# Attention's transposes moved from VectorE to the DMA queue, and the down/wo weight sums made in place inside the first gate/up pass

## Chip, cores and metric

The kernel runs on 1 core of one Trainium2 chip. The metric is device time in microseconds (us), the median over runs. Before the change it is 732.66 us, the median of 6 runs (731.0 to 733.2).

## What is computed

A gated mix of two branches over 2048 tokens of width 1024. `B` is a gated feed-forward block (hidden width 3584). `A` is a sliding, dilated attention: 32 heads of 32, each token looks at 8 keys, 0, 2, ..., 14 positions back. A sigmoid gate per token mixes them. Cut to what matters:

```python
def _A_ref(x, wqkv, wo):
    H = 32; Dh = D // H; W, dil = 8, 2
    q, k, v = split_heads(x @ wqkv)
    idx = pos[:, None] - (jnp.arange(W) * dil)[None, :]
    mask = idx >= 0
    logits = jnp.einsum("bhsd,bhswd->bhsw", q, k[idx]) * Dh ** -0.5
    attn = softmax(jnp.where(mask, logits, -1e9))
    o = jnp.einsum("bhsw,bhswd->bhsd", attn, v[idx])
    return merge_heads(o) @ wo

def _B_ref(x, w_gate, w_up, w_down):
    return (gelu(x @ w_gate) * (x @ w_up)) @ w_down

g = sigmoid((x * gate_w).sum(-1, keepdims=True))
out = g * _A_ref(x, wqkv, wo) + (1 - g) * _B_ref(x, w_gate, w_up, w_down)
```

## The kernel before

**Tiling.** The 2048 tokens are four chunks of 512 (`SC`); two chunks form a "sup". For each sup the program runs a gate/up pass (`ffn`, L963: 28 tiles of 128 hidden columns, taken two at a time as 14 blocks) and then a down stage for each of its chunks (`down`, L1063 and `down_rest`, L1136). In between stands the q, k, v projection of the next sup's chunks (`qkv_pair`); the first two chunks are projected at the start (`qkv_outer`, `qkv`). The large products are made by a scheme of seven half-size products instead of eight (Strassen's, in Winograd's form), in pairs of chunks or halves. It needs sums and differences of the operands beforehand: of the gate/up weights (`wforms`, L427), of x (`x_forms`), of the projection weights (`qkv_forms`), of the down and wo weights (`preps`, L402) and of h (`forms`, L1095), all made by VectorE. The sums of down and wo weights are stored to DRAM (`dforms`, `oforms`) by DMAs on the POOL queue and read back in each down stage; the gate/up sums are used at once and also stored (`fforms`) for the second sup.

**Attention.** It has no matmuls besides the projections. A chunk is taken as two halves of 256 tokens, so there are eight halves, `h` = 0 to 7. `scores` (L765) multiplies q by eight shifted views of k on VectorE and adds over eight tiles: eight products (L781) and seven adds (L787), each of 128 x 2048 bf16. `att_half` (L818) then has partial sums with the head's channels on the partitions. It transposes them (L844), folds the four remaining channels (L851, L854), takes the softmax over the eight window positions (L867 to L898, with the exponential on ScalarE, L880), spreads the weights back over channels on ScalarE (L904), transposes back in two pieces (L913), multiplies by eight shifted views of v (L922) and sums over the window (L930, L935, L939). The result overwrites q in `qo` and is the left operand of the wo product in the down stage. The transposes are VectorE's, by blocks of 32 x 32, so that a partition after the transpose holds one token of a group of 32 and 8 heads; the gate's per-token values `ez` and the mask follow that layout (`SB`, `HQ`, L861).

Five buffers `xbuf` (128 x 2048 bf16) serve all of it. The products of half `h` wait until the transpose of half `h`-1 is done (`acct`, L772).

**Weights.** `ring` has 20 slots of 256 KB. Every weight piece is loaded into the next free slot by a DMA on SP's queue; a slot is free when the last matmul on it is done. SP issues strictly in order: `loads` (L366) is the list. A block of the first gate/up pass takes four loaded pieces and four sums, a block of the second seven loads, a product of the down stage nine pieces.

**The order.** `Weave` (L41) puts several generators (`main`, `loads`, `wforms`, `preps`, `attention`, `scores` and others) into one order for each engine when the program is built: it keeps a clock per engine, gives every operation a written cost, and always emits the operation that could start first, plus a small bias per generator (L1255). The order is fixed then; each engine works through its own list and waits at whichever operation isn't ready. A DMA is taken to end when its bytes have passed a pipe of 340 GB/s and 2.2 us more have gone (L90 to L93). The operations of `main` stay in order among themselves.

**`preps` and its staging.** Nine rounds: seven for the down weights, two for wo. A round loads four 256 KB pieces (`load_prep`, L316), makes four differences of 128 x 1024 (L409 to L414), and stores four pieces (L419). The loads go to one of five areas in rows 8 to 27 of `hT`, the results to the next area (L405). `hT` is the hidden activation (28 rows), which the gate/up pass fills from row 0 up; rows from 8 on wait until all of `preps` is stored (L1030). The loads of all nine rounds stand before block 2's in the list.

Of the kernel before, what the change touches and what calls it, by code (L numbers as in the profile page):

```python
# [9 lines left out]
ALU = mybir.AluOpType  # L10
# [30 lines left out]
class Weave:  # L41
# [42 lines left out]
    def _emit(self, op, t):  # L84
        cost = op.cost
        if op.eng == "ACT" and op.table is not None and op.table != self.table:
            self.table = op.table
            cost += 1.29
        if op.eng in ("SP", "POOL"):
            nbytes, issue = op.cost  # L90
            self.clk[op.eng] = t + issue
            self.pipe = max(self.pipe, t) + nbytes / self.RATE
            op.end = self.pipe + 2.2  # L93
        else:
            self.clk[op.eng] = t + cost
            op.end = t + cost + op.tail
        instructions = self.nc.cur_bb.bb.instructions
        n0 = len(instructions)
        op.fn()
        for ins in self.nc.cur_bb.bb.instructions[n0:]:  # L100
            eng = getattr(ins, "engine", None)
            if eng is None or not getattr(ins, "name", None) or type(ins).__name__.startswith("BassTile"):
                continue
            prev = self.last.get(eng)
            if prev is not None:
                self.tc.add_manual_dep(ins, prev, mybir.DependencyInfo(mybir.DependencyClass.NoSync,
                                                                      mybir.DependencyReason.DATA),
                                       reason="engine order")
            self.last[eng] = ins.name
            self.names.append((ins.name, len(self.log)))  # L110
        if op.key is not None:
            self.done[op.key] = op
        self.log.append((op.eng, t, op.end, op.key, op.fn.__qualname__.split(".")[2], op.cost))
# [23 lines left out]
def kernel(  # L137
# [31 lines left out]
    SB = AC // 32  # L169
    HQ = 32 // DL  # L170
# [126 lines left out]
    NPREP = FH + NTH  # L297
    def stage(i):
        f0 = 8 + 4 * i
        return hT[:, :, f0:f0 + 4, :].rearrange("p (a b) f s -> p a b (f s)", b=2)  # L300
# [14 lines left out]

    def load_prep(i0):  # L316
        n = min(2, NPREP - i0)
        kind, src, nr = ("d", B_w_down, FH) if i0 < FH else ("o", A_wo, NTH)
        r0 = i0 if kind == "d" else i0 - FH
        si = i0 % 5  # L320

        def fn():
            st = stage(si)
            for h, r in ((0, r0), (1, nr + r0)):
                if kind == "d":
                    v = src[r * P:(r + n) * P, :].rearrange("(k p) (h n) -> p k h n", p=P, h=2)
                else:
                    v = AP(src.tensor, src.offset + r * D, [[NT * D, P], [D, n], [NW, 2], [1, NW]])
                for k in range(n):
                    nc.sync.dma_start(out=st[:, 2 * h + k], in_=v[:, k])  # L330
        return Op("SP", (4 * n * P * NW * 2, 2.0 * n), fn, [("preps", i0 - 6)] if i0 >= 6 else [], key=("prep", i0))
# [34 lines left out]
    def loads():  # L366
# [5 lines left out]
                 [("pt", NST - 1, 1)], key=("wqkv", 0, 2))  # L372
        yield load_prep(2)
        yield from load_x(1, [])
        for i0 in (4, 6, 8, 10):
            yield load_prep(i0)
        yield from load_block(0, 0)
        yield load_prep(12)
        yield from load_block(0, 1)
        for i0 in (14, 16):  # L380
            yield load_prep(i0)
        for b in range(2, NBLK):
            yield from load_block(0, b)
            if b >= XB:
                for c, k0 in ((2, 0), (2, 4), (3, 0), (3, 4))[b - XB:b - XB + 1]:
                    yield from list(load_x(c, []))[k0:k0 + 4]
# [15 lines left out]
    def preps():  # L402
        for i0 in range(0, NPREP, 2):
            kind, r0, n = ("d", i0, min(2, FH - i0)) if i0 < FH else ("o", i0 - FH, min(2, NPREP - i0))
            st, ot = stage(i0 % 5), stage((i0 + 1) % 5)  # L405
            b11, b12, b21, b22 = st[:, 0:n, 0], st[:, 0:n, 1], st[:, 2:2 + n, 0], st[:, 2:2 + n, 1]
            fo = ot[:, :, 0:n, :]
            t = tt(n * NW)
            f0 = dve(t, lambda: V(out=fo[:, 0], in0=b12, in1=b11, op=ALU.subtract), [("prep", i0)], lag=1.0)  # L409
            yield f0  # L410
            yield dve(t, lambda: V(out=fo[:, 2], in0=b22, in1=b12, op=ALU.subtract))
            f1 = dve(t, lambda: V(out=fo[:, 1], in0=b22, in1=fo[:, 0], op=ALU.subtract), [f0])
            yield f1
            last = dve(t, lambda: V(out=fo[:, 3], in0=b21, in1=fo[:, 1], op=ALU.subtract), [f1])  # L414
            yield last
            dd = (ddram if kind == "d" else odram)[:].rearrange("f p (k n) -> p f k n", n=NW)
            for f in range(4):
                o = Op("POOL", (n * P * NW * 2, 0.8),
                       lambda f=f: nc.gpsimd.dma_start(out=dd[:, f, r0:r0 + n, :], in_=fo[:, f]), [last],  # L419
# [289 lines left out]
    def gate(c):  # L709
# [20 lines left out]
        ez = small.tile([P, SC // 32], F32, tag="ez", bufs=2, name="ez")  # L730
        omg = small.tile([P, NST], F32, tag="omg", bufs=3, name="omg")
        gates[c] = (ez, omg, zq)

    def gate_sum(c):
        i, free = bank_take()
        zq = gates[c][2]

        def go():
            for q in range(4):
                nc.tensor.matmul(banks[i][32 * q:32 * (q + 1), 0:SC // 32], lhsT=qsum[:], rhs=zq[:], start=True, stop=True,  # L740
# [3 lines left out]
        e = dve(0.1, lambda: nc.vector.tensor_scalar(out=zq[:], in0=banks[i][:, 0:SC // 32], scalar1=ZMAX, scalar2=-ZMAX,  # L744
# [4 lines left out]
    def gate_tail(c):  # L749
        ez, omg, og = gates[c]  # L750

        def tail():
            nc.vector.tensor_scalar(out=og[:], in0=ez[:], scalar1=1.0, scalar2=1.0, op0=ALU.mult, op1=ALU.add)
            nc.vector.reciprocal(out=og[:], in_=og[:])
            for q in range(4):
                nc.vector.tensor_copy(out=omg[32 * q:32 * (q + 1), :],
                                      in_=og[32 * q:32 * (q + 1), :].rearrange("p (j q) -> p j q", q=4)[:, :, q])
        yield dve(1.2, tail, [("ez", c)], lag=0.6, key=("omg", c))
# [6 lines left out]
    def scores():  # L765

        for c in range(NCH):
            q_, k_ = qo[c % 2], kT[c]
            for a in range(SC // AC):
                a0 = a * AC  # L770
                h = (SC // AC) * c + a
                gate_ = [("acct", h - 1)] if h else []  # L772
# [45 lines left out]
    def att_half(c, a, h):  # L818
# [12 lines left out]

        def lsb():
# [8 lines left out]
        def attn():  # L841
            return flat("w")[:, 3 * CW:4 * CW].rearrange("p (w c) -> p w c", w=NWIN)

        o = dve(2.24, taking("z", lambda: nc.vector.transpose(out=flat("z"), in_=xbuf[:, accs[h], :])), [("qk", h)],  # L844
                pre=xb_pre(), key=("acct", h))
# [11 lines left out]
        if h == 0:  # L857
            def mask():
                for q in range(4):
                    for wi in range(1, NWIN):  # L860
                        nc.vector.memset(lsb()[32 * q:32 * q + DIL * wi, wi, 0:HQ], NEG)  # L861
            o = dve(2.0, mask, [o])
# [14 lines left out]
        def exps():  # L877
            if a == 0:
                nc.scalar.activation(out=gates[c][0][:], in_=gates[c][2][:], func=ACT.Exp)
# [4 lines left out]
        if a == 0:  # L884
# [7 lines left out]
                                .to_broadcast([P, SB, HQ]), op=ALU.mult), [("ez", c), o])  # L892
# [18 lines left out]
        for i in range(2):  # L911
            def back(i=i):
                nc.vector.transpose(out=flat("ab")[:, i * n // 2:(i + 1) * n // 2],  # L913
                                    in_=flat("e")[:, i * n // 2:(i + 1) * n // 2])
            o = dve(1.16, taking("ab", back) if i == 0 else back, [es[i]], lag=0.6, pre=xb_pre() if i == 0 else None)
# [47 lines left out]
    def ffn(sup, mid, early=()):  # L963
# [29 lines left out]
        for i in range(FT + 2):  # L993
# [33 lines left out]
            if 1 <= i < FT + 1:  # L1027
                f = i - 1
                o = yield from prod(Bk[f], 2, T3, f, False, [ev[f, "u2"]])
                d = [("stored", "o")] if (sup == 0 and f >= 8) else []  # L1030
# [224 lines left out]
    w.run([(0.0, main()), (0.0, loads()), (0.1, wforms()), (0.1, x_forms()), (0.1, qkv_forms()), (0.15, preps()), (0.3, attention()), (0.5, scores())])  # L1255
# [31 lines left out]
```

## Time and profile before

| | |
|---|---|
| median of 6 runs | 732.66 us |
| the profiled execution, its own time | 731.19 us |
| its span, first to last instruction | 729.4 us |
| clock granted to TensorE | 0.999 |
| DMA queues, bytes moved | 163.73 MB, mean 224 GB/s |
| VectorE, transposes L844 | 8 of 2.306 us (median) |
| VectorE, transposes L913 | 16 of 1.234 us (median) |
| VectorE, sums L409 to L414 | 9 rounds, 14.7 to 91.7 us |
| SP, weight pieces L362 | 252 DMAs of 256 KB, 4.8 us from issue to landing (median) |

Where the stages lie, from the chain of waits and the timeline (us from the span's start):

| stage | from | to |
|---|---|---|
| projections of chunks 0 and 1 | 8.0 | 92.2 |
| first gate/up pass | 92.7 | 260 to 274, woven with the next |
| down, chunk 0 | 260 | 314 |
| projections of chunks 2 and 3 | 314 | 390 |
| down, chunk 1 | 390 | 445 |
| second gate/up pass | 445 | 613 to 625, woven with the next |
| down, chunks 2 and 3 | 613 | 725.8 |

The answers quoted below read as follows. A line of the list of waits: engine and line that waited, what released it; total us, times, longest. A line of the timeline: start, length in us, engine, line, operation, out<-in, count; in brackets the idle time before it and what ended it. A line of a tile or source line: count, then shortest/median/longest duration in ns, first and last start. A line of a stretch: its limits and length, then busy us of TensorE's matmuls, its weight loads, VectorE, ScalarE and POOL, each with its count, then the granted clock, the DMA engines' busy share and GB/s. `PE` is TensorE, `DVE` VectorE, `ACT` ScalarE, `SPq` the queue of SyncE.

### The profile page before, as it was taken

Reading aid. Unit: us, or ns where it says so; the run is one execution under the profiler, and the core shown is the slowest. Engines: PE = TensorE matmul, PEld = TensorE weight load, DVE = VectorE, ACT = ScalarE, POOL = GpSimd, SP = SyncE. Lnnn points to the kernel's source line nnn. Section 1 sums busy time; section 2 is a strip of 40 time slices with the busy share of each in tenths; the row PEclk is TensorE's granted clock in tenths of the full one; section 3 lists DMA queues with packets and bytes.
Section 4 is the critical chain, followed back from the end, with each engine's and each line's share of the span. In section 5 each row is a group of like instructions: output and inputs, shape, how many; then the busy total and the mean of one; then the engine's idle time right before and its main releaser. Section 6 shows DMA issues by size and latency. Waiting matters only on the chain.

```text
span 729.4 us, 9904 instructions
## 1 busy us (share of the span) xinstructions
PE 717.7 (98%) x3330; PEld 355.8 (49%) x3397; DVE 631.1 (87%) x935; ACT 314.9 (43%) x532; POOL 72.2 (10%) x128
## 2 busy tenths in 40 slices
PE   8999999999999999999999998999999999999997
PEld 5666644444444444456665443444444444444443
DVE  2689999999999989999899999999999999969300
ACT  2333455558555561035652113576557654220110
POOL 2234422111210100000000001000000000001000
PEclk9999999999999999999999999999999999999999
DMA  8999965648892769943129999555555544899992
GB/s 303 326 323 360 380 212 166 194 132 216 213 227 79 275 203 322 321 151 107 37 91 314 344 303 336 163 152 154 147 158 147 157 150 145 305 304 336 320 309 99
DMA packets 151507, 163.73 MB, mean 224 GB/s; under 512 B 22944, under 2 KB 112032, under 8 KB 151456
## 3 DMA queue, kind: packets, MB, share of 16 engines
q1 hardware_dynamic: 142624, 135.30, 61.0%
q0 software_dynamic: 8544, 27.27, 10.0%
q8 instruction: 26, 0.43, 0.3%
q10 hardware_dynamic: 288, 0.52, 0.2%
q14 instruction: 25, 0.20, 0.1%
HBM read 129.50 MB, written 28.31 MB: 216 GB/s over the span
## 4 chain that ended last, share of the span: by engine, by line
PE 72%; issue 22%; DVE 2%; DMA 2%; ACT 1%; POOL 1%; POOLq 0%; ACTq 0%
PE ps L970 44%; PE ps L1117 16%; PE ps L473 11%; DVE xbuf L922 1%; POOL out_dram L1144 1%; DMA ring<-in_B_w_down_dram 1%; DMA hT<-in_A_x_dram 0%; DVE xbuf L930 0%; PE ps L1212 0%; DMA out_dram<-ost 0%; DVE xbuf L935 0%; DVE ost L1191 0%; ACT ost L1152 0%; ACT L1058 0%; DVE xbuf L787 0%
## 5 line engine op out<-in xcount | busy, mean ns | idle before, releaser
L970 PEld LDWEIGHTS <-ring 128*128 128x128 bf16 x1568 | 153.2, 98 | 187.7 <-issue 3.5
L970 PE MATMUL ps<-lend,ring 128*128 128x512 bf16 x878 | 210.4, 379 | 3.1 <-ACT m L1024 2.1
L970 PE MATMUL ps<-tf,ring 128*128 128x512 bf16 x658 | 162.6, 379 | 0.8
L1117 PE MATMUL ps<-ring,hT 128*128 128x512 bf16 x693 | 159.7, 379 | 0.8
L1117 PEld LDWEIGHTS <-hT 128*128 128x128 bf16 x708 | 69.2, 98 | 83.3
L781 DVE TENSOR_TENSOR xbuf<-qo,lend 128x2048 bf16<-128x2048 bf16 x64 | 77.4, 1218 | 2.2 <-ACT lend L495 2.2
L922 DVE TENSOR_TENSOR xbuf<-xbuf,lend 128x2048 bf16<-128x2048 bf16 x64 | 77.4, 1219 | 0.1
L787 DVE TENSOR_TENSOR xbuf<-xbuf 128x2048 bf16<-128x2048 bf16 x56 | 68.2, 1218 | 0.2
L609 PEld LDWEIGHTS <-ring 128*128 128x128 bf16 x336 | 44.0, 131 | 28.7 <-DMA ring<-in_A_wqkv_dram 0.4
L473 PE MATMUL ps<-lend,ring 128*128 128x512 bf16 x250 | 55.5, 380 | 0.4
L999 ACT COPY ps<-ps 128x512 f32<-128x512 f32 x56 | 32.0, 571 | 54.9 <-PE ps L970 54.8
L1042 ACT ACTIVATE gl<-ps 128x512 bf16<-128x512 f32 x56 | 33.5, 598 | 50.6 <-PE ps L970 50.6
L1152 ACT ACTIVATE ost<-ps,omg 128x512 bf16<-128x512 f32 x16 | 11.0, 688 | 102.5 <-PE ps L1117 99.3
L1144 POOL DMA_DIRECT2D out_dram<-ost x24 | 13.0, 542 | 413.4 <-ACT ost L1152 319.4
L1117 PE MATMUL ps<-ring,qo 128*128 128x512 bf16 x187 | 48.7, 379 | 0.2
L473 PEld LDWEIGHTS <-ring 128*128 128x128 bf16 x256 | 36.7, 144 | 18.8 <-DMA hT<-in_B_w_down_dram 0.4
L443 POOL DMA_DIRECT2D fforms<-ring x56 | 30.5, 545 | 131.9 <-DVE ring L435 122.8
L609 PE MATMUL ps<-lend,ring 128*128 128x512 bf16 x187 | 43.0, 379 | 0.4 <-issue 0.2
L1014 DVE TENSOR_TENSOR hT<-hT,gl 128x1024 bf16<-128x1024 bf16 x56 | 38.4, 686 | 5.7 <-ACT hT L1011 4.5
L930 DVE TENSOR_TENSOR xbuf<-xbuf 128x1024 bf16<-128x1024 bf16 x64 | 41.9, 687 | 0.7
L1054 DVE TENSOR_TENSOR u<-ps,u 128x512 f32<-128x512 f32 x56 | 38.4, 686 | 4.4 <-PE ps L970 3.3
L1033 DVE TENSOR_TENSOR hT<-ps,m 128x512 bf16<-128x512 f32 x56 | 38.4, 686 | 3.7 <-PE ps L970 3.7
(106 smaller groups left out, 724.5 us busy)
## 6 DMA issues: line engine op xcount, KB each, us to landing
ring<-dforms SPq DMA_DIRECT2D x112, 256.0 KB, 4.7
ring<-in_B_w_down_dram SPq DMA_DIRECT2D x84, 256.0 KB, 4.1
ring<-in_B_w_gate_dram SPq DMA_DIRECT2D x56, 256.0 KB, 4.7
fforms<-ring POOLq DMA_DIRECT2D x56, 256.0 KB, 4.9
ring<-fforms SPq DMA_DIRECT2D x56, 256.0 KB, 3.8
ring<-in_B_w_up_dram SPq DMA_DIRECT2D x42, 256.0 KB, 3.3
ring<-in_A_wqkv_dram SPq DMA_DIRECT2D x40, 256.0 KB, 4.9
ring<-oforms SPq DMA_DIRECT2D x32, 256.0 KB, 5.5
```

The costliest lines, as they stand in the source:

```text
L473: nc.tensor.matmul(banks[bk][:], lhsT=lhsT, rhs=xT(c, kt), start=(kt == 0), stop=(kt == KT - 1))
L609: nc.tensor.matmul(banks[bk][:], lhsT=lhsT, rhs=rhs[:, kt, :], start=(start and kt == 0), stop=(kt == KH - 1), skip_group_check=True)
L781: V(out=w3(box[t]), in0=q_b, in1=k_w, op=ALU.mult)
L787: V(out=w3(box[0]), in0=w3(box[0]), in1=w3(box[t]), op=ALU.add)
L922: return dve(tt(n), taking(("p", t), lambda: V(out=w3(box["p", t]), in0=w3(box["ab"]), in1=v_w, op=ALU.mult)), [("qkv", c, 2, t), abo] + ( ...
L930: V(out=s4(t)[:, t % 2], in0=w3(box["p", t])[:, 0:4], in1=w3(box["p", t])[:, 4:8], op=ALU.add)
L970: nc.tensor.matmul(banks[bk][:], lhsT=wv[:, k, fl * P:(fl + 1) * P], rhs=rhs[:, k, :], start=(start and k == 0), stop=(k == KH - 1), skip_ ...
L1014: yield dve(tt(2 * SC), lambda f=f: nc.vector.tensor_tensor(out=hT[:, :, f, :], in0=hT[:, :, f, :], in1=gl[f][:].rearrange("p (j s) -> p j ...
L1033: ev[f, "up2"] = dve(tt(SC, True), lambda f=f: nc.vector.tensor_tensor(out=hs(f, 1), in0=v3(banks[Bk[f]][:]), in1=v3(m5[f][:]), op=ALU.add ...
L1042: nc.scalar.activation(out=gl[f][:, SC:2 * SC], in_=banks[A[f]][:], func=ACT.Gelu_apprx_tanh)
L1054: e = dve(tt(SC, True), lambda f=f: nc.vector.tensor_tensor(out=u2[f][:], in0=banks[Dk[f]][:], in1=u2[f][:], op=ALU.add), [o, ev[f, "u2"]])
L1117: nc.tensor.matmul(banks[bk][:], lhsT=l, rhs=wv[:, i, :], start=(start and k == 0), stop=(q == last and i == 1), skip_group_check=True)
```

## The change

The transposes L844 and L913 become DMA transposes on SP's queue: one of 512 KB from `xbuf` to `xbuf` for each half on the way in, and two of 256 KB on the way back. They transpose whole blocks of 128 x 128, so a partition afterwards holds one token of a group of 128 and all 32 heads. The gate's values, the mask and the gate's matmul follow: 4 columns instead of 16, and no copies by quarter at the end. The products of the next half wait for the last add of the half before (`qk`) instead of its transpose (`acct`). `Weave` adds an operation's `tail` to a DMA's end where it is over 1 us; the new DMAs have such tails.

`preps` works in place, in three areas in rows 16 to 27 of `hT`; only rows from 16 on wait for the stores. In the list of loads, rounds stand after blocks 0, 2, 3, ... 7, one at a time, and the load of chunk 1's x moves ahead of the second round. The x loads of chunks 2 and 3 become a stream of their own, `late_x`.

```diff
-            op.end = self.pipe + 2.2
+            op.end = self.pipe + 2.2 + (op.tail if op.tail > 1.0 else 0.0)
...
-    SB = AC // 32
-    HQ = 32 // DL
+    SB = AC // P
...
+    NSTG = 3
     def stage(i):
-        f0 = 8 + 4 * i
+        f0 = FT - 4 * (i + 1)
...
+    def late_x():
+        for i in range(4):
+            yield from list(load_x(2 + i // 2, [("w", 0, XB + i, 3)]))[4 * (i % 2):4 * (i % 2) + 4]
...
-        return Op("SP", (4 * n * P * NW * 2, 2.0 * n), fn, [("preps", i0 - 6)] if i0 >= 6 else [], key=("prep", i0))
+        return Op("SP", (4 * n * P * NW * 2, 2.0 * n), fn, [("preps", i0 - 2 * NSTG)] if i0 >= 2 * NSTG else [], key=("prep", i0))
...
+        yield from load_x(1, [])
         yield load_prep(2)
-        yield from load_x(1, [])
-        for i0 in (4, 6, 8, 10):
-            yield load_prep(i0)
         yield from load_block(0, 0)
-        yield load_prep(12)
+        yield load_prep(4)
         yield from load_block(0, 1)
-        for i0 in (14, 16):
-            yield load_prep(i0)
         for b in range(2, NBLK):
             yield from load_block(0, b)
-            if b >= XB:
-                for c, k0 in ((2, 0), (2, 4), (3, 0), (3, 4))[b - XB:b - XB + 1]:
-                    yield from list(load_x(c, []))[k0:k0 + 4]
+            if 4 + 2 * (b - 1) < NPREP:
+                yield load_prep(4 + 2 * (b - 1))
...
-            fo = ot[:, :, 0:n, :]
+            fo = (b11, b22, b12, b21)
-            f0 = dve(t, lambda: V(out=fo[:, 0], in0=b12, in1=b11, op=ALU.subtract), [("prep", i0)], lag=1.0)
+            f0 = dve(t, lambda: V(out=b11, in0=b12, in1=b11, op=ALU.subtract), [("prep", i0)], lag=1.0)
...
-                nc.tensor.matmul(banks[i][32 * q:32 * (q + 1), 0:SC // 32], lhsT=qsum[:], rhs=zq[:], start=True, stop=True,
+                nc.tensor.matmul(banks[i][32 * q:32 * (q + 1), 0:NST], lhsT=qsum[:],
+                                 rhs=zq[:].rearrange("p (j q) -> p j q", q=4)[:, :, q], start=True, stop=True,
...
-            for q in range(4):
-                nc.vector.tensor_copy(out=omg[32 * q:32 * (q + 1), :],
-                                      in_=og[32 * q:32 * (q + 1), :].rearrange("p (j q) -> p j q", q=4)[:, :, q])
-        yield dve(1.2, tail, [("ez", c)], lag=0.6, key=("omg", c))
+        yield dve(0.3, tail, [("ez", c)], lag=0.6, key=("omg", c))
...
-                gate_ = [("acct", h - 1)] if h else []
+                gate_ = [("qk", h - 1)] if h else []
...
+        def turn(cols, fn, deps, **kw):
+            return Op("SP", (P * cols * 2, max(1.3, cols / 1000.0)), fn, deps, tail=4.0 if h == 0 else 1.1, lag=1.0, **kw)
...
-        o = dve(2.24, taking("z", lambda: nc.vector.transpose(out=flat("z"), in_=xbuf[:, accs[h], :])), [("qk", h)],
-                pre=xb_pre(), key=("acct", h))
+        o = turn(n, taking("z", lambda: nc.sync.dma_start_transpose(out=rows("z"), in_=xbuf[:, accs[h], :])), [("qk", h)],
+                 pre=xb_pre(), key=("acct", h))
...
-                nc.vector.transpose(out=flat("ab")[:, i * n // 2:(i + 1) * n // 2],
-                                    in_=flat("e")[:, i * n // 2:(i + 1) * n // 2])
-            o = dve(1.16, taking("ab", back) if i == 0 else back, [es[i]], lag=0.6, pre=xb_pre() if i == 0 else None)
+                nc.sync.dma_start_transpose(out=rows("ab")[:, i * NWIN:(i + 1) * NWIN],
+                                            in_=flat("e")[:, i * n // 2:(i + 1) * n // 2])
+            o = turn(n // 2, taking("ab", back) if i == 0 else back, [es[i]], pre=xb_pre() if i == 0 else None)
...
-                d = [("stored", "o")] if (sup == 0 and f >= 8) else []
+                d = [("stored", "o")] if (sup == 0 and f >= FT - 4 * NSTG) else []
...
-    w.run([(0.0, main()), (0.0, loads()), (0.1, wforms()), (0.1, x_forms()), (0.1, qkv_forms()), (0.15, preps()), (0.3, attention()), (0.5, scores())])
+    w.run([(0.0, main()), (0.0, loads()), (0.0, late_x()), (0.1, wforms()), (0.1, x_forms()), (0.1, qkv_forms()), (0.15, preps()), (0.3, attention()), (0.5, scores())])
```

## The prediction

> **What bounds the kernel now.** Read first: the page's busy shares, then the list of who waited for whom on TensorE, then the timeline around the one long wait. The span is 729.4 us, the profiled run 731.19 us, so 1.8 us lie around the span; the median of the runs shown, 732.66, lies 1.47 us above that run.
>
> ```profile
> PE 717.7 (98%) x3330; PEld 355.8 (49%) x3397; DVE 631.1 (87%) x935; ACT 314.9 (43%) x532; POOL 72.2 (10%) x128
> ...
> PE ps L970 <- ACT m L1024: 2.1, 1, 2.1
> PE ps L279 <- DVE hT L277: 1.2, 1, 1.2
> PE ps L1212 <- DMA hT<-in_A_x_dram: 0.8, 1, 0.8
> PE ps L609 <- issue: 0.2, 1, 0.2
> ```
>
> TensorE works nearly all the time. Of its four waits two (1.2 and 0.8 us) are in the start, before any line that the change touches. So only 2.1 + 0.2 = 2.3 us can be won; the 42 us of VectorE work that goes away are no gain in themselves. The 2.1 us:
>
> ```profile
> 448.58 1.89 PE L970 MATMUL ps<-lend,ring 128*128 128x512 bf16 x8
> ...
> 452.90 1.03 PE L970 MATMUL ps<-tf,ring 128*128 128x512 bf16 x4
> 456.00 1.89 PE L970 MATMUL ps<-lend,ring 128*128 128x512 bf16 x8 [2.08 <-ACT m L1024]
> ...
> 454.13 0.68 DVE L1054 TENSOR_TENSOR u<-ps,u 128x512 f32<-128x512 f32 x1
> ...
> 454.85 0.63 ACT L1058 ACTIVATE gl<-u 128x512 bf16<-128x512 f32 x1 [3.77 <-DVE u L1054]
> ```
>
> The first four of the eight matmuls at 448.58 end at about 449.6 and make L1054 ready; VectorE reaches it at 454.13, 4.5 us late, behind attention work it was still draining. ScalarE stands in line at L1058, its copy L1024 behind it is late, TensorE loses 2.08 us. So at this place a late evacuation is forgiven up to 4.5 - 2.1 = 2.4 us. I use this slack below for the whole gate/up pass, as an estimate.
>
> ```profile
> L913 DVE STREAM_TRANSPOSE xbuf<-xbuf x16: 1201/1234/1245, 92.3 to 647.1; 128x1024 bf16<-128x1024 bf16 x16
> L844 DVE STREAM_TRANSPOSE xbuf<-xbuf x8: 2300/2306/2311, 62.4 to 621.5; 128x2048 bf16<-128x2048 bf16 x8
> ...
> L313 SPq DMA_TRANSPOSE lend<-in_A_x_dram x24: 1124/1282/2556, 26.0 to 217.7; - x24
> DMA to landing us min/median/max: 2.6/4.9/8.0
> ...
> 25.95 12.99 SPq L313 DMA_TRANSPOSE lend<-in_A_x_dram  x8
> ...
> 52.00:92.00 40.00, 39.70 (x189) 26.36 (x191) 38.73 (x90) 16.06 (x27) 18.81 (x29) 1.00 1.08 374
> 92.00:190.00 98.00, 97.45 (x456) 44.12 (x466) 95.90 (x139) 60.14 (x103) 19.49 (x35) 1.00 0.62 183
> ...
> 390.00:445.00 55.00, 54.74 (x265) 24.98 (x270) 54.28 (x75) 9.94 (x17) 3.79 (x7) 1.00 0.98 326
> ```
>
> These show what is removed, the only DMA transposes the kernel has so far (128 KB each), and three stretches (their last column is GB/s): DMA is full before the first gate/up pass, half free inside it, full again in the down stage.
>
> [...] here four such blocks (L313) take 1.28 us of the queue, 0.32 us each[...]. [...] eight of 128 KB took 12.99 us, 81 GB/s. [...] SP waits at L313 for VectorE, up to 2.0 us. So each new transpose that waits for VectorE or ScalarE holds all weight loads behind it on SP.
>
> **The change part by part.**
>
> *VectorE.* Gone: 8 x 2.306 + 16 x 1.234 = 38.2 us of transposes; the four small copies of the gate tail (0.69 us a chunk, 2.8 in all); 21 of 28 mask memsets of 65 ns (1.4). Together 42.4 us, some 4.8 us per half chunk. In the order of the new kernel the work that stood before L1054 in the second pass is shorter: all adds of that half now stand before the forms of the down stage. In the trace the forms end at 412.9; fold to second scale, with the score products between, is then about 15.7 us by the rows' durations (to about 429), and from the last output evacuation (due about 437) 11.9 us of attention stand before the first evacuation of the pass: 437 + 0.7 + 11.9 = 449.6, when it is due. The stall goes: -2.1 us. Next late there is the landing of the transposes below.
>
> *The transposes as DMAs.* 24 new issues on SP, 1 MB per half chunk. The trace has no SBUF-to-SBUF transpose, so I bound it. Below: 512 KB at the 374 GB/s of the second stretch, 1.4 us, plus the least landing of L313, 2.6: 4.0 us. Above: 16 blocks x 0.32 = 5.1 us on the queue plus L313's landing after its queue time, 4.9 - 1.3 = 3.6: 8.7 us. I take the middle, 6.3. The cover is what VectorE has in line between the last add of a half and the fold that needs the result, summed from the new order with the rows' durations (1.14 for a 2048-wide product, 0.61 for an evacuation, by start spacing): halves 0 to 6: 7.4, 8.5, 8.2, 8.1, 11.8, 7.6, 5.2 us; half 7 has 1.8 us of work, but these are evacuations that TensorE paces, about 4.6 us. At 6.3 us the last two are late by 1.1 and 1.7, inside the 2.4: nothing lost. The way back is two pieces of 256 KB: second piece at most 1.5 + 2.6 + 3.6 = 7.7 us after its copy, covers 5.4 to about 12 us: late by 2.3 at most. Cost taken: 0; ends: 0 and, if landings exceed the upper bound, the slower rival.
>
> *SP behind them.* In the down stage SP waits for TensorE to free slots anyway (L362 on L1117, 82.4 us in 122 waits, up to 3.5 us, one long wait per product). A piece's slot is free some 12 us before it is needed (20 slots, 9 pieces a product, 3.9 us a half product), landing takes 4.8: 7 us to spare. One transpose takes 1.4 to 5.1 us of it. Cost 0; its cover gone, see the third rival. In the gate/up passes the ring is over 20 us ahead.
>
> *Weight sums.* Same operations: 9 rounds of four 0.686 us subtractions, in place; the order shows three rounds before the first pass and six (16.5 us) in it, with their 4 loads and 4 stores of 256 KB per round. DMA per block: 16 x 0.262 MB = 4.19 MB in the 12.1 us of 56 matmuls = 347 GB/s, against 374 seen; before it was 173, as the 183 of the row says. VectorE's sum is the same: what leaves 52 to 92 us lets attention start earlier. On POOL 24 issues of 0.54 us go among the form stores; it is 10% busy. The last round must be stored before row 16 of h is written, at about 92.7 + 17 x 6.05 = 195 us; its load goes behind block 7, some two blocks ahead of TensorE's 177 us: near 155, plus 6 for loading, 3 of sums, 6 of storing = 170, 25 us early. Cost 0, upper end 2 us if a load holds VectorE past the 2.4.
>
> *Small edits with one answer:* the second x load before the second round, x of the later chunks as its own stream, gate sums of 4 columns for 16: TensorE's order is otherwise unchanged; hidden.
>
> Sum against the profiled run: 731.19 - 2.1 = 729.1; at the median 732.66 - 2.1 = 730.6.
>
> **Rivals.** (1) *Given back*: the stall goes, but several landings come 2.5 to 3 us late. For it: 24 new waits, VectorE 96 to 99% busy in those stretches. Against: the covers. Four losses of 0.4 us: 732.2, no change. (2) *Slower: the landing outruns the cover.* Place: the fold of halves 1, 2, 5, 6 and 7 in the gate/up passes, with an evacuation right behind it. It decides from a landing of 5.2 + 2.4 = 7.6 us on. L313 has landed 3.1 us above its median; the upper bound plus that is 11.8; at 10 us half 6 loses 10 - 7.6 = 2.4, halves 1 and 2 end just inside, half 7 loses 3.0, and the second pieces some 2 more: 730.6 + 7.4 = 738.0; at 8.7 it is 1.1 + 1.7: 733.4. Typical 736. (3) *Weights late:* the transposes take the DMA engines as L313 does, 16 x 0.32 x 2 = 10.3 us a half; three halves fall into down stages at 0.86 to 0.98 share, each with 7 us to spare: 3 x 3.3 = 10: 740. Against: one transpose comes at a time, a product or more apart. (4) The sums don't fit into the 27 GB/s left (347 of 374) beside half 1's transposes: like (3), but with 25 us of slack; within its chance.
>
> **Numbers.** Forecast 0.48, its own range 729.2 to 731.2; given back 0.17; landing 0.25; weights or sums 0.10. A change under 0.2% (1.5 us) can't be told from none. So faster 0.48, same 0.17, slower 0.35. The range 729.0 to 738.5 leaves out most of (3) and (4) and the far part of (2), together under 0.2.
>
> **What would show it.** Right: no TensorE wait on L1024 near 454, TensorE's waits under 0.5 us beside the start's, VectorE near 590 us. Landing: VectorE rows of the fold and the first product with idle time released by a DMA on xbuf, and TensorE waits after them. Weights: TensorE released by a DMA on ring in the down stages or at 92 to 190 us. Wrong altogether: a TensorE wait in the projections before 92 us.

## The result, and the profile after

The changed kernel takes 730.01 us (median of 18 runs, 728.84 to 732.17), the kernel before beside it 732.17 us (36 runs, 730.64 to 733.73). The ratio is 0.9973, with an interval of 0.9965 to 0.9981: faster by 0.27%, some 2.2 us. The profiled execution of the changed kernel took 730.68 us, its span is 728.9 us.

The two profiled executions differ by only 731.19 - 730.68 = 0.5 us, the medians by 2.2. The rest is in how the profiled executions stand to their medians: before's lies 1.0 below its own, after's 0.7 above. The last experiment bears on the first part of that; the second is not explained.

The page of the changed kernel, its busy shares (busy us, share of the span, instructions):

```profile
PE 717.7 (98%) x3330; PEld 355.2 (49%) x3397; DVE 593.2 (81%) x874; ACT 315.7 (43%) x533; POOL 72.4 (10%) x128
```

Its list of waits on TensorE (total us, times, longest):

```profile
PE ps L278 <- DVE hT L276: 1.2, 1, 1.2
PE ps L973 <- DMA ring<-in_B_w_up_dram: 0.7, 1, 0.7
PE ps L1215 <- DMA hT<-in_A_x_dram: 0.6, 1, 0.6
PE ps L472 <- DMA ring<-in_A_wqkv_dram: 0.6, 2, 0.4
PE ps L973 <- ACT m L1027: 0.4, 1, 0.4
PE ps L973 <- DVE hT L1036: 0.2, 1, 0.2
PE ps L608 <- issue: 0.2, 1, 0.2
```

TensorE is exactly as busy as before. The wait of 2.1 us on the copy (L1024 then, L1027 now) is gone. New are three waits at L973, in the first pass, of 1.3 us together, and 0.6 us at the start. The start's waits cost nothing in the end, for the first pass begins at 92.61 us here and at 92.64 before. From there the starts of TensorE's matmuls give the account. The projections of chunks 2 and 3 begin at 319.81 us instead of 318.08, so the first pass and the first down stage lose 1.8 us. From the start of the second pass to the last group of matmuls it takes 724.25 - 446.85 = 277.4 us instead of 724.78 - 445.13 = 279.65, so 2.25 us are won. Together that is the 0.5 us by which the two spans differ.

The timeline of the changed kernel where the stall was:

```profile
450.30 1.89 PE L973 MATMUL ps<-lend,ring 128*128 128x512 bf16 x8
...
455.48 1.89 PE L973 MATMUL ps<-lend,ring 128*128 128x512 bf16 x8
...
452.26 0.68 DVE L1057 TENSOR_TENSOR u<-ps,u 128x512 f32<-128x512 f32 x1
...
452.98 0.63 ACT L1061 ACTIVATE gl<-u 128x512 bf16<-128x512 f32 x1 [0.19 <-DVE u L1057]
```

The group at 450.30 answers to the one at 448.58 before. Its first four matmuls end near 451.3, and VectorE makes the evacuation at 452.26, 0.9 us later instead of 4.5. ScalarE waits 0.19 us behind it instead of 3.77, and TensorE goes from group to group without a gap.

The new transposes, from the lines' own view (count, shortest/median/longest time on the queue in ns, first and last start; then issue to landing, and who waited). First the way in of the changed kernel, then the way back:

```profile
L848 SPq DMA_TRANSPOSE xbuf<-xbuf x8: 1908/3212/4297, 56.8 to 602.3; - x8
...
  DVE xbuf L855: 2.9, 3
...
DMA to landing us min/median/max: 4.3/5.7/8.3
```

```profile
L916 SPq DMA_TRANSPOSE xbuf<-xbuf x16: 1231/1300/3213, 76.7 to 626.9; - x16
...
  DVE xbuf L925: 4.3, 2
...
DMA to landing us min/median/max: 3.0/5.6/7.6
```

VectorE waited for 24 transposes only five times, 7.2 us in all, and no evacuation of the second pass was late enough for TensorE to see it. The three waits at the fold (L855) are those of halves 2, 4 and 7 (0.45, 0.61 and 1.82 us). It is just these three transposes that SP issued late, 4.3, 4.9 and 1.2 us after the last add of the half, because other entries of its queue stood ahead.

The stretches of the changed kernel that answer to those shown of before (limits and length, busy us of TensorE, its weight loads, VectorE, ScalarE, POOL; clock, DMA share, GB/s):

```profile
52.00:92.00 40.00, 39.70 (x189) 26.35 (x191) 39.30 (x61) 15.53 (x27) 8.19 (x14) 1.00 0.66 189
92.00:190.00 98.00, 96.19 (x449) 43.35 (x458) 90.82 (x143) 58.67 (x100) 33.34 (x53) 1.00 0.91 284
...
390.00:445.00 55.00, 54.74 (x266) 25.32 (x270) 48.35 (x66) 10.17 (x17) 3.79 (x7) 1.00 1.08 330
```

The sums' traffic has moved: 374 GB/s became 189 before the first pass, and 183 became 284 inside it. There TensorE lost 97.45 - 96.19 = 1.3 us. The down stage, with DMA at 1.08, lost nothing (54.74 as before). How the first pass loses its time, from the timeline of the changed kernel:

```profile
134.49 1.22 DVE L785 TENSOR_TENSOR xbuf<-xbuf 128x2048 bf16<-128x2048 bf16 x1
...
147.08 0.69 DVE L434 TENSOR_TENSOR ring<-ring 128x1024 bf16<-128x1024 bf16 x1 [0.81 <-DMA ring<-in_B_w_up_dram]
149.47 0.69 DVE L434 TENSOR_TENSOR ring<-ring 128x1024 bf16<-128x1024 bf16 x1 [1.69 <-DMA ring<-in_B_w_gate_dram]
...
161.78 2.61 DVE L434 TENSOR_TENSOR ring<-ring 128x1024 bf16<-128x1024 bf16 x4
...
164.91 0.68 DVE L1036 TENSOR_TENSOR hT<-ps,m 128x512 bf16<-128x512 f32 x1
...
135.74 3.39 SPq L848 DMA_TRANSPOSE xbuf<-xbuf  x1
139.23 1.37 SPq L346 DMA_DIRECT2D ring<-in_B_w_up_dram  x2
...
163.10 1.89 PE L973 MATMUL ps<-lend,ring 128*128 128x512 bf16 x8 [0.43 <-ACT m L1027]
165.65 1.89 PE L973 MATMUL ps<-tf,ring 128*128 128x512 bf16 x8 [0.67 <-DMA ring<-in_B_w_up_dram]
```

SP stands at half 1's transpose until VectorE has made the last add (134.49 + 1.22 = 135.7). Block 6's weights go out only behind it, at 139.2 (135.45 before). The first to need them is VectorE, which makes the weight sums L434 of block 6 from 147 us on and waits 0.81 and 1.69 us for them. TensorE comes to block 6 only at about 166 us, so no piece is late for TensorE. Its small waits are for evacuations. For the longest, 0.67 us, the profile names a DMA of weights, but the pieces on their way then (issued from 160.11 on) belong to block 8; TensorE goes on at 165.65, when VectorE ends L1036 (164.91 + 0.68 = 165.59). In two other executions of the same first pass (the kernels with doubled transposes below) this wait is 0.67 us again and ends 0.06 us after the same evacuation. So VectorE is late there. That its 2.5 us of waits at 147 us are what makes it late is the likely reading; no run shows it alone.

### The profile page after: what moved, and what is told of

It is laid out like the page before. It is cut to its first block, busy times and chain, and to the rows that moved or that the text cites. A ratio compares the mean times of both kernels' runs of the same rounds, so it can differ in the third digit from the quotient of the medians.

```text
span 728.9 us, 9922 instructions
## 1 busy us (share of the span) xinstructions
PE 717.7 (98%) x3330; PEld 355.2 (49%) x3397; DVE 593.2 (81%) x874; ACT 315.7 (43%) x533; POOL 72.4 (10%) x128
## 4 chain that ended last, share of the span: by engine, by line
PE 92%; DMA 5%; ACT 1%; issue 1%; SPq 0%; DVE 0%; DVEq 0%; ACTq 0%
PE ps L973 43%; PE ps L1120 29%; PE ps L608 10%; PE ps L472 9%; DMA ring<-in_A_wqkv_dram 2%; DMA ring<-in_B_w_gate_dram 1%; DMA hT<-in_B_w_down_dram 1%; DMA ring<-in_B_w_up_dram 1%; DMA ring<-dforms 1%; PE ps L716 0%; SPq L307 0%; ACT L1061 0%; ACT L882 0%; SPq L274 0%; DVE ring L434 0%
## 5 line engine op out<-in xcount | busy, mean ns | idle before, releaser
L973 PEld LDWEIGHTS <-ring 128*128 128x128 bf16 x1568 | 153.2, 98 | 187.3 <-issue 3.2
L973 PE MATMUL ps<-lend,ring 128*128 128x512 bf16 x878 | 210.4, 379 | 1.4 <-ACT m L1027 0.4
L973 PE MATMUL ps<-tf,ring 128*128 128x512 bf16 x658 | 162.6, 379 | 1.7 <-DMA ring<-in_B_w_up_dram 0.7
L1017 DVE TENSOR_TENSOR hT<-hT,gl 128x1024 bf16<-128x1024 bf16 x56 | 38.6, 689 | 12.8 <-ACT hT L1014 11.8
L1036 DVE TENSOR_TENSOR hT<-ps,m 128x512 bf16<-128x512 f32 x56 | 38.4, 687 | 4.1 <-PE ps L973 3.9
```

What stands on the lines that cost most here:

```text
L973: nc.tensor.matmul(banks[bk][:], lhsT=wv[:, k, fl * P:(fl + 1) * P], rhs=rhs[:, k, :], start=(start and k == 0), stop=(k == KH - 1), skip_ ...
L1017: yield dve(tt(2 * SC), lambda f=f: nc.vector.tensor_tensor(out=hT[:, :, f, :], in0=hT[:, :, f, :], in1=gl[f][:].rearrange("p (j s) -> p j ...
L1036: ev[f, "up2"] = dve(tt(SC, True), lambda f=f: nc.vector.tensor_tensor(out=hs(f, 1), in0=v3(banks[Bk[f]][:]), in1=v3(m5[f][:]), op=ALU.add ...
```

## The experiments

The theory after the result: the gain is one place, the first evacuation of the second pass, which half 4's lighter work brings forward; the rest of the change is hidden or costs, and the cost comes from half 1's transpose and the sums in the first gate/up pass. Rivals: the gain is spread over all halves; the sums' new place brings it; a simple hold of SP explains the loss. The changed kernel was not run again beside these kernels, so a difference from it goes by the ratios, each taken to the kernel before in its own group of runs.

**All transposes, without the sums' new place.** `preps`, its loads and the x loads stay as before.

```diff
+            op.end = self.pipe + 2.2 + (op.tail if op.tail > 1.0 else 0.0)
-        o = dve(2.24, taking("z", lambda: nc.vector.transpose(out=flat("z"), in_=xbuf[:, accs[h], :])), [("qk", h)],
+        o = turn(n, taking("z", lambda: nc.sync.dma_start_transpose(out=rows("z"), in_=xbuf[:, accs[h], :])), [("qk", h)],
```

> The DMA transposes alone, with the weight sums as they were (five areas, before the pass). If the gain is VectorE's lateness at the start of the second gate/up pass: that wait of 2.1 us is gone and the time is about 730.0, ratio to before 0.997. If the gain comes from the sums' new place: 732, ratio 1.000. If the sums cost something where they now stand, this kernel is below the changed one by 0.3 to 1.3 us.

Measured 749.41 us (745.78 to 752.21), ratio 1.0232 (1.0205 to 1.0259): slower by 17 us. From its timeline:

```profile
80.11 0.69 DVE L855 TENSOR_TENSOR xbuf<-xbuf 128x1024 bf16<-128x1024 bf16 x1 [6.25 <-DMA xbuf<-xbuf]
...
101.86 1.86 PE L973 MATMUL ps<-lend,ring 128*128 128x512 bf16 x4 [6.42 <-ACT ps L1002]
...
229.51 12.39 SPq L312 DMA_TRANSPOSE lend<-in_A_x_dram  x4
242.00 1.08 SPq L341 DMA_DIRECT2D ring<-in_B_w_up_dram  x2
...
256.66 1.89 PE L973 MATMUL ps<-tf,ring 128*128 128x512 bf16 x4 [10.07 <-DVE ring L434]
```

Two new stalls. The first: half 0's transpose goes out while the sums' transfers fill the DMA engines (1.07 share from 52 to 92 us) and lands after 17.4 us, the longest of the eight; VectorE idles 6.25 us at the fold, and everything behind it, the first evacuations included, is late. The second: the x loads stand in the weights' list as before, now wait for attention that runs differently, and take 12.39 us for four; the last block's weights go out at 242 and TensorE waits 10.07 us. So two parts of the change that I had put down as costing nothing seem to be what makes the rest possible; a later run takes up the x loads.

**The sums alone,** with x as its own stream, and VectorE's transposes.

```diff
-        f0 = 8 + 4 * i
+        f0 = FT - 4 * (i + 1)
-            fo = ot[:, :, 0:n, :]
+            fo = (b11, b22, b12, b21)
-                d = [("stored", "o")] if (sup == 0 and f >= 8) else []
+                d = [("stored", "o")] if (sup == 0 and f >= FT - 4 * NSTG) else []
```

> The weight sums in place inside the first pass (and the x loads' new order) alone, transposes on VectorE. If the gain is VectorE's lateness: the wait near 454 us stays, 732 to 734, ratio 1.000 to 1.003. If the gain is the sums' place: about 730, ratio 0.997.

Measured 733.25 us (21 runs), ratio 1.0023 (1.0013 to 1.0033), 1.5 us slower. The wait of the second pass stays (1.6 us) and a second one appears in the first pass; from the list of waits on TensorE of this kernel:

```profile
PE ps L970 <- ACT m L1024: 3.7, 2, 2.0
```

The new place of the sums brings nothing by itself, and with VectorE's transposes it has a price of its own of about 1.5 us. An evacuation in the first pass is late (2.05 us at 103.84). Of the 16.5 us of sums in this pass only one round stands ahead of it (four differences, 95.67 to 99.25 us); the rest of VectorE's work there is half 0's attention and weight sums. So the late evacuation comes from what now stands ahead of it in VectorE's list, of which the sums are a part.

**Only half 4 by DMA,** all else as before. The gate's values for this half keep the old layout: the kernel leaves the change of layout out, so its output is not the right one.

```diff
+DMAH = (4,)
+        if h in DMAH:
+            o = turn(n, taking("z", lambda: nc.sync.dma_start_transpose(out=rows("z"), in_=xbuf[:, accs[h], :])), [("qk", h)],
+                     pre=xb_pre(), key=("acct", h))
```

> The kernel before with one half of eight (half 4, the one that ends at the stall) transposed by DMA; that half's gate values and mask are in the other layout, so its numbers change and its work does not. If only what stands ahead of the late evacuation counts, 4.8 us less there against 4.5 us of lateness: the whole gain, 730.0 to 730.3, ratio 0.997. If the lateness is pooled over several halves, only part: 731 to 732.

Measured 728.44 us (728.07 to 729.37), ratio 0.9958 (0.9944 to 0.9972). One half of eight brings more than the whole change, and no wait of 0.2 us in the gate/up passes or the down stages is left. Its waits on TensorE:

```profile
PE ps L474 <- DMA ring<-in_A_wqkv_dram: 1.9, 2, 1.3
PE ps L280 <- DVE hT L278: 1.2, 1, 1.2
PE ps L1230 <- DMA hT<-in_A_x_dram: 0.4, 1, 0.4
```

The rival of a spread gain falls. But VectorE's list is not the old one with less in it. `Weave` has made a new order, and VectorE idles 6.00 us before the fold (at 425.10) and 6.29 us before half 4's products with v. These are L922 in the kernel before and L940 here; first a line of before, then two of this kernel:

```profile
452.99 1.22 DVE L922 TENSOR_TENSOR xbuf<-xbuf,lend 128x2048 bf16<-128x2048 bf16 x1
```

```profile
450.19 2.36 DVE L940 TENSOR_TENSOR xbuf<-xbuf,lend 128x2048 bf16<-128x2048 bf16 x2 [6.29 <-DMA xbuf<-xbuf]
452.47 0.68 DVE L1072 TENSOR_TENSOR u<-ps,u 128x512 f32<-128x512 f32 x1
```

In before all eight of these products stand ahead of the first evacuation (the line shown is the eighth); here two do, and six follow it. In the changed kernel it is seven. So the stall's end is shown to come with half 4's transposes on the DMA queue, but in this kernel the evacuation is early by the new order, not by 4.8 us of work less. Whether that order would do it with VectorE's transposes was not tried.

**Half 1's transpose later on SP,** behind block 6's loads, in the changed kernel.

```diff
-            return Op("SP", ..., tail=4.0 if h == 0 else 1.1, lag=1.0, **kw)
+            return Op("SP", ..., tail=4.0 if h == 0 else 1.1, lag=6.0 if h == 1 else 1.0, **kw)
```

> The changed kernel with the first transpose of half 1 placed on SP behind the next block's weight loads. If SP's wait for VectorE there (about 4.5 us) makes block 6's weights late, TensorE's 1.3 us of waits between 150 and 166 us go and the time is about 729.0 to 729.4. If the DMA engines are simply full there (4.19 MB a block), it stays at 730.0.

Measured 732.73 us (22 runs), ratio 1.0017 (1.0005 to 1.0028): slower than the changed kernel by 2.7 us (by the ratios 3.2) instead of faster by about one. From its timeline:

```profile
160.18 0.69 DVE L855 TENSOR_TENSOR xbuf<-xbuf 128x1024 bf16<-128x1024 bf16 x1 [3.89 <-DMA xbuf<-xbuf]
...
164.33 1.89 PE L973 MATMUL ps<-lend,ring 128*128 128x512 bf16 x8 [1.43 <-ACT m L1027]
...
167.27 1.89 PE L973 MATMUL ps<-tf,ring 128*128 128x512 bf16 x8 [1.05 <-DVE hT L1036]
```

The weights do go out earlier (136.17 instead of 139.23), and VectorE no longer waits for block 6's. But now the transpose starts at 143.76, is 7.8 us on the queue and lands after 16.4; VectorE waits 3.89 us for this fold (6.8 us in three for all folds instead of 2.9), and the evacuations behind it are late. So this run does not show that the hold of SP causes the loss: in this stretch the order of SP decides what VectorE waits for, the weights or the fold.

**Some transposes made twice** in the changed kernel, first halves 5 and 6 (second gate/up pass), then halves 4 and 7 (in the down stages).

```diff
-        o = turn(n, taking("z", lambda: nc.sync.dma_start_transpose(out=rows("z"), in_=xbuf[:, accs[h], :])), [("qk", h)],
+        o = turn(n, taking("z", lambda: [nc.sync.dma_start_transpose(out=rows("z"), in_=xbuf[:, accs[h], :])
+                                         for r in range(2 if h in (5, 6) else 1)]), [("qk", h)],
```

> The changed kernel with the way-in transpose of halves 5 and 6 done twice, the second after the first has landed, so that their results come some 5.7 us later (about 11.4 in all). Both lie in the second gate/up pass, where the weights are far ahead. If a late evacuation is forgiven 2.4 us beyond the cover of 7.6 and 5.2 us: +1.4 and +3.8, together about 5 us over the changed kernel, 735. If the landing doesn't matter because VectorE has idle time enough: at most +0.5.

> The same doubling for halves 4 and 7, whose way-in transposes stand among the weight loads of down stages. If 7 us of spare lead cover it: half 4 nothing (cover 11.8), half 7 up to 2: 730 to 732. If weights come late behind a held queue or full DMA engines: 3 us or more, with TensorE waits released by a DMA on ring.

Halves 5 and 6: 731.07 us (12 runs), ratio 0.9989 (0.9979 to 1.0), about 1 us above the changed kernel, not 5. VectorE's waits at the fold rise (7.8 us in five instead of 2.9 in three), but TensorE loses only 0.6 us in the pass (busy 166.42 of 168 us against 167.04). Halves 4 and 7: 735.47 us (4 runs), ratio 1.0061 (1.0046 to 1.0076), 5.5 us above by the medians, 6.4 by the ratios. The waits of the second kernel, on TensorE and on VectorE:

```profile
PE ps L974 <- ACT m L1028: 2.1, 1, 2.1
...
PE ps L1121 <- DMA ring<-dforms: 1.2, 4, 0.4
```

```profile
DVE xbuf L856 <- DMA xbuf<-xbuf: 11.0, 3, 6.2
```

So the forecast's rivals exist, but behind a reserve. Inside a gate/up pass one more transpose of 512 KB for each of two halves is nearly swallowed. For halves 4 and 7 it isn't. Half 4's two copies hold SP from 403.75 to 412.88 us, in a down stage; its weights then come late in four places (1.2 us), and the stage ends 2.9 us later against its start than in the changed kernel. Half 7's fold waits 6.2 us, and TensorE waits 2.1 us for an evacuation at 617.76, where the second pass ends.

**All transposes, and x as its own stream;** this is the first experiment with this one thing changed.

```diff
+DMAC = (0, 1, 2, 3)
+    def late_x():
+        for i in range(4):
+            yield from list(load_x(2 + i // 2, [("w", 0, XB + i, 3)]))[4 * (i % 2):4 * (i % 2) + 4]
-            if b >= XB:
-                for c, k0 in ((2, 0), (2, 4), (3, 0), (3, 4))[b - XB:b - XB + 1]:
-                    yield from list(load_x(c, []))[k0:k0 + 4]
```

> The transposes alone, as in the first run, but with the x loads of chunks 2 and 3 as a stream of their own instead of in line with the weights. If SP, held at those x loads until attention is done, made the last block's weights late (TensorE's wait of 10.1 us at 256.7): that wait goes, 736 to 740. The wait of 6.4 us at 101.9 stays, being half 0's landing among the sums' transfers. If the two waits have one cause (full DMA engines): both shrink or both stay, 745 to 750.

**The same without chunk 0** (halves 0 and 1 stay on VectorE).

```diff
-DMAC = (0, 1, 2, 3)
+DMAC = (1, 2, 3)
```

> As the run with x as its own stream, but chunk 0 (halves 0 and 1) back on VectorE, sums before the pass as they were. If half 0's slow landing among the sums' transfers was the rest of the loss: both waits gone, 728.5 to 730, ratio 0.996 to 0.997. If other halves lose too: 731 or more.

With all chunks 736.77 us, ratio 1.0071 (1.0046 to 1.0096): the stall of 10.07 us is gone, that at the start of the first pass is still there (3.9 us; longest landing 14.9 us). Moving the sums as well turns this kernel into the changed one, at 0.9973. Without chunk 0 728.66 us, ratio 0.9961 (0.9947 to 0.9975). The waits on TensorE over 0.2 us of the kernel without chunk 0:

```profile
PE ps L281 <- DVE hT L279: 1.2, 1, 1.2
PE ps L1249 <- DMA hT<-in_A_x_dram: 0.6, 1, 0.6
PE ps L612 <- DVE qo L673: 0.4, 1, 0.4
PE ps L476 <- DMA ring<-in_A_wqkv_dram: 0.4, 1, 0.4
```

Nothing is left in the gate/up passes. What the changed kernel loses in the first pass is thus due to chunk 0's transposes and the sums that moved for their sake, taken together; neither is needed for the gain.

**Only chunk 2, and only chunks 2 and 3,** with sums and loads as before.

```diff
-DMAC = (1, 2, 3)
+DMAC = (2,)
```

> The kernel before with chunk 2 alone (halves 4 and 5) transposed by DMA, gate values and mask of that chunk in the new layout. If the gain is what stands ahead of one late evacuation: as half 4 alone, 728.2 to 728.8, ratio 0.996, better than the changed kernel. If each further half by DMA adds a loss of its own: 729 to 730.

> The kernel before with chunks 2 and 3 (halves 4 to 7) by DMA. If transposes in the second pass are hidden: 728.2 to 728.8, as chunk 2 alone. If they cost something each: 729 to 730.

728.70 us, ratio 0.9956 (0.9941 to 0.9971), and 728.95 us, ratio 0.9960 (0.9945 to 0.9974). With the two above they are one group of 728.4 to 729.0, some 3 us under the kernel before and, by the ratios, about 1 us under the changed kernel; the intervals of the single ratios overlap with the changed kernel's. Chunk 2 (halves 4 and 5) is all that is needed; more transposes by DMA add nothing that can be seen. In these kernels, as with half 4 alone, only two of half 4's eight products with v stand ahead of the first evacuation.

**The kernel before, profiled twice more,** without any edit, because its times spread over 3 us while those of the last group spread over less than 2.

> The kernel before, unchanged, profiled once more. The times of before spread from 730.6 to 733.7, and its profile (own time 731.19) is near the low end, so the stall of 2.1 us in it may be a mild case. Theory A (the stall varies): in an execution whose own time is T, TensorE's wait near 454 us on the copy L1024, together with what follows it, is 2.1 + (T - 731.2): about 3.6 us at the median 732.2 to 732.7, and the other waits stay as they were. Theory B (something else varies): the stall is 2.1 us again within 0.3, and a higher own time shows as other TensorE waits, at the start or in the first gate/up pass, or lies outside the span (own time less span over 1.9 us).

> The kernel before once more, for a second execution of the same; as in the run before: theory A has the stall near 454 us grow with the own time (2.1 us at 731.2, 3.6 at 732.7), theory B has it at 2.1 within 0.3 whatever the own time is.

The first of the two profiled executions took 731.43 us, the second 733.60. In both the wait is 2.1 us, as in the first profile. What differs comes right behind it. The second one's timeline:

```profile
456.71 3.40 PE L970 MATMUL ps<-lend,ring 128*128 128x512 bf16 x8 [2.07 <-ACT m L1024]
459.91 2.11 PE L970 MATMUL ps<-tf,ring 128*128 128x512 bf16 x8
```

and its stretches there, with the columns as above:

```profile
457.00:460.00 3.00, 3.00 (x9) 1.08 (x8) 2.96 (x6) 0.64 (x2) 0.00 (x0) 0.50 0.76 233
460.00:463.00 3.00, 3.00 (x15) 1.31 (x14) 1.45 (x3) 2.18 (x4) 0.00 (x0) 0.94 0.24 59
```

Eight matmuls that take 1.89 us in the other two profiles take 3.40 here, and the next eight 2.11: the granted clock is 0.50 for 3.4 us after the gap. That costs 1.5 + 0.2 = 1.7 us on top of the 2.1. Theory A, which counted what follows the stall with it, is the nearer: 3.8 us of the 4.5 it gives for 733.6. The stall itself doesn't vary, as theory B had it, but no other wait appears.

The record tells how often this happens. Half the clock for 3.4 of 731.8 us lowers the mean clock to 0.998. Of 110 executions of the kernel before whose mean clock is on record, 47 have 0.997 or 0.998, and they take 732.0 to 733.9 us (median 732.9); the other 63 have 0.999 or 1.000 and a median of 731.1. The medians differ by 1.8 us, about the 1.7 of the one profiled. Of the changed kernel's 18 executions none is under 0.999. That the low clock of all 47 lies behind the stall is likely and not shown.

## Why the prediction was right, point by point

- *The stall goes, -2.1 us.* Right, and in the changed kernel for the stated reason: VectorE has idle time in the down stage (2.1 and 3.2 us), makes its last output evacuation there at 439.59 us, 7.3 us before the pass begins (before 440.92, 4.2 us), and from its end to the first evacuation of the pass lie 12.0 us of attention (440.25 to 452.26), where 11.9 were forecast. The evacuation is 0.9 us late instead of 4.5, less than the 2.4 that are forgiven. Half 4 alone does it, which the prediction didn't separate, but there by another order of VectorE's list.
- *Sum against the profiled run, 729.1 us; at the median 730.6.* The profiled run is 730.68: 1.6 off. The median is 730.01: 0.6 off. That the median agrees so well is in part luck, for two errors of opposite sign nearly cancel. The cost taken as 0 was 1.8 us in the profiled execution. And the stall was worth more than the 2.3 us that "can be won", which counted waits alone: where half a clock follows the stall it costs 1.7 us more, and 20 of the 36 runs of before lie over 732 us.
- *Landing of the way in, 6.3 taken, 4.0 to 8.7 as bounds.* Measured 4.3 to 8.3 with a median of 5.7: inside. On the queue 3.2 us (median), between the 1.4 and 5.1. The way back landed after 5.6 (at most 7.6, where 7.7 was the bound).
- *The covers, and 2.4 us of slack.* The landings were counted from the last add of a half. The time until SP gets to the transpose was left out: 4.9 us for half 4, whose cover of 11.8 us was therefore not enough (wait 0.61), 4.3 for half 2 and 1.2 for half 7. The longest landing, 8.3 us, was half 1's and inside its cover of 8.5. By the prediction's own figures half 7 (4.6 + 2.4 = 7.0 us), not half 6, decides rival 2; it came 1.8 us late, inside the slack. The slack was too small an estimate for the middle of the pass: with halves 5 and 6 doubled the time rose by 1 us where 5 was expected.
- *"In the gate/up passes the ring is over 20 us ahead", SP's hold at no cost.* The lead is right for TensorE: block 6's weights went out at 139.2, some 26 us before TensorE came to them. The conclusion failed in the first pass, because there VectorE needs the pieces first, for the weight sums; it waited 2.5 us for them at 147 us. The evacuations behind it were late for TensorE by up to 0.67 us.
- *Weight sums, "Cost 0, upper end 2 us".* The size failed, the bound held: alone they cost 1.5 us. I checked DMA (347 GB/s worked out for a block; 341 seen from 116 to 164 us) and the last round, but not what would stand ahead of the first evacuations of the pass. The old stores (L419) took 0.73 us each to issue, not 0.54; POOL is 10% busy all the same.
- *"The second x load before the second round, x of the later chunks as its own stream ... hidden".* In the changed kernel nothing shows of it, but it isn't a small edit: without it the new order of the attention held the weights and cost a stall of 10.07 us.
- *Weights late, the third rival.* Didn't come, though DMA reached 1.08 in the down stage. With the transposes of halves 4 and 7 doubled it came, 1.2 us in four places of one down stage.
- *VectorE near 590 us.* 593.2: 37.9 us went, of 42.4 (the copies were 2.6 us, not 2.8; the rest of the difference isn't traced). *TensorE's waits under 0.5 us beside the start's.* 1.3 + 0.2 = 1.5: this sign was missed, by the first pass. *"Wrong altogether: a TensorE wait in the projections before 92 us."* There are two, 0.6 us on projection weights, so this sign did show. It was badly chosen: the first pass begins no later for them, and the two kernels with doubled transposes don't have them.
- *Two readings of before.* The 81 GB/s of the x transposes are this queue's share: in these 13 us the DMA engines were full (1.23) and moved 276 GB/s in all, so the transposes' own rate isn't in this trace. SP's longest wait for VectorE at L313 is 2.4 us, not 2.0.

What stays open: whether a new order of VectorE's list would end the stall without any DMA transpose, and how the loss of the first pass divides into SP's order, full DMA engines and VectorE's order (the one attempt to move a part made it worse). How large this loss is can be told from three executions with the same first pass: from its start to the projections of chunks 2 and 3 TensorE takes 227.2, 226.4 and 226.8 us, against 225.2 to 225.4 in the three of the kernel before. That is 1.0 to 2.0 us.

## What to carry to other kernels

When an engine is 98% busy, look for its few waits and free just those: of eight halves only one mattered, the one whose attention work stood ahead of the first evacuation of a pass. Where a program orders the operations, an edit changes the order too, so compare what stands ahead of the late operation before and after, and don't credit the work that was removed. In these runs a transfer that waited for a compute engine also held what stood behind it on SP's queue: SP stood 4.5 us at half 1's transpose, and block 6's weights went out at 139.23 us behind it, at 136.17 where they stood ahead. Price such a transfer by the next loads on its queue in each stage, and by the engine that needs them first. Count its own landing from the time when the queue gets to it, which was up to 4.9 us after the last add here. And a gap of 2.07 us on TensorE cost 3.8 us in one of three profiled executions, so read several before a stall is priced.

## What the runs showed of the hardware

- A gap of about 2.1 us on TensorE was followed in one of three profiled executions of the kernel before by 3.4 us at a granted clock of 0.50 (0.50 from 457 to 460 us, 0.94 from 460 to 463), and in the other two by none (1.00 from 454 to 463). In other kernels the clock was below 1 around longer gaps as well: 0.95 from 90 to 98 us and 0.84 from 98 to 106 with the gap of 3.94 us that ends at 97.86, in the kernel with x as its own stream; 0.57 from 98 to 106 with the gap of 6.42 us that ends at 101.86, and 0.50 from 250 to 258 and 0.71 from 258 to 266 with the gap of 10.07 us that ends at 256.66, in the first experiment.
- Why the same gap lowered the clock in one execution and not in the other two was not shown.
- In these runs SBUF to SBUF DMA transposes took less time for a block than those from DRAM: 512 KB in 3.2 us on the queue (median of 8 in the changed kernel), about 0.2 us a block of 128 x 128, where the x loads took 0.32 in pieces of 128 KB (1.28 us, median of 24 in the kernel before). With a DMA share of 1.07 from 52 to 92 us, in the first experiment, one landed after 17.4 us; the median in the changed kernel is 5.7.
